# Dealing out the output projection between scores in a two-layer attention and gated-unit kernel

## The chip, the core and the metric

The kernel runs on one core of one Trainium2 chip. Its time is the device time in microseconds of one execution. Below, TensorE (PE) multiplies matrices, VectorE (DVE) and ScalarE (ACT) work on elements and may read PSUM, GpSimd (POOL) works on elements in SBUF and issues some DMAs, SyncE (SP) issues most DMAs. Each engine takes its own instructions in order. PSUM is where matmuls leave their sums; here it is used as eight banks of 128 x 512 float32.

## The reference

Two attention layers and two gated-unit layers alternate on x of 2048 rows and 448 columns. The weights of the two attention layers are the same, and so are those of the two gated units. There are 16 heads of 28 columns, which share one key and one value (multi-query attention).

```python
q = (x @ wq).reshape(B, S, H, Dh).transpose(0, 2, 1, 3)
k = x @ wk
v = x @ wv
p = _softmax(jnp.einsum("bhqd,bkd->bhqk", q, k) * (Dh ** -0.5))
attention = einsum("bhqk,bkd->bhqd", p, v) -> (B, S, H * Dh), then @ wo
unit = (_sigmoid(x @ w_gate) * (x @ w_up)) @ w_down

x = x + attention(_layernorm(x))
x = x + unit(_layernorm(x))
x = x + attention(_layernorm(x))
x = x + unit(_layernorm(x))
```

## The kernel before

**Precision.** Operands are split into a high and a low float16 part; a product is the sum of three of the four part products (high by high, high by low, low by high). Hence the output projection of one tile is 4 x 3 = 12 matmuls of 448 columns (line 625), and similar triples stand elsewhere.

**Tiles and steps.** The rows are 16 tiles of 128 (index `u`). The keys are 16 tiles of 128 (`kt`). A layer's attention is a loop of 16 x 16 steps. In a step, the order of the instructions is the string `ORDER = "FSFSFSFSPXM"`:

- `S`, four times: one score matmul of 128 keys by 4 heads x 128 rows into a PSUM bank (line 523), then the exponential on ScalarE into SBUF (line 526).
- `P`: the product with the values of the step before, eight TensorE records into one PSUM bank of its own (line 534).
- `X`: `tick()`, which counts down the stages of tiles whose attention is done, and issues those that are due; and the new rate of the filling work.
- `M`: one group of the row maxima of a later tile: four matmuls (line 493, `mx`), each into its bank, and four reductions on VectorE (line 497, `mp`).
- `F`, four times: `fill.slice`, which advances the count `now`, issues the work that was deferred (`defer`, `flush`), and then takes matmuls from the filling generators until a debt in ns is paid. The costs are constants (190 for 448 columns, 110 for 256, 216 for 512). The filling work is the gated unit of earlier rows (gate and up products `gp`, `up` at line 353, down products `dn` at line 716) and, in places, the query projection (`qp`).

**PSUM.** One bank holds the values' sums. The other seven have one tag, and all of `s`, `mx`, `gp`, `up`, `dn`, `qp`, `wo`, `mt` take theirs from it.

**Maxima.** The exponential needs each row's maximum ahead of the scores. It goes into the scores as row 28 of the query tile `QS`. When the 16 groups of a tile are done (24 for the first tile of the second layer), the generator `mx_gen` goes on at its next call: it reduces over the groups and scales (lines 506 and 507, `m32`, `m16`), puts a function `fin` into the list `late`, and begins the next tile's first group, ahead of which `fin` is called. `fin` transposes on TensorE (line 512, `mt`), copies on VectorE (line 514) and writes the row into `QS` by a DMA of GpSimd. `mx_gen` also issues the loads of `QH` (line 460) and the twelve loads of `QS` (line 449) on SyncE.

**After a tile's attention.** `Block.tile` (line 570) lists the stages of a tile with the number of steps to wait ahead of each: `f0` and `fx` store the row sums and load them in another shape; `fy` takes the reciprocal on VectorE (line 591); `fz` and `fw` store it and load it across the partitions; `fa` multiplies on GpSimd (line 608); `fb` splits into float16 parts on ScalarE and VectorE (lines 614, 615); `fc` is the output projection, twelve matmuls in one go, and defers the addition of the residual and the statistics (lines 630, 301, 302; then six operations on GpSimd); `fd` norms (lines 330, 322 to 324) and, for a block's second tile, loads the first two weight tiles; `fe` transposes by DMA (line 341); `ff` counts the tile as fed. Two tiles make a block; when both are fed, the block's gated unit becomes filling work. `FIRST` tells the planner at which step the first block is fed, and so how fast the filling has to go. What `tick()` issues directly (`fill.run`) is charged to the debt, which later slices pay by taking less.

In the first layer the weights are prepared beside all this (`paced`), and the stages `fa` and `fb` of its first four tiles wait two steps each. At a layer's end a loop of rounds (one `tick` and four slices) runs what is left; `KEEP` keeps filling work back for it.

Of the kernel before, what the change touches and what calls it, by code (L numbers as in the profile page):

```python
# [19 lines left out]
def interleaved_layers_kernel(ctx: ExitStack, tc: tile.TileContext, x, wq, wk, wv, wo, wg, wu, wd, out, layers=2):  # L20
# [45 lines left out]
    def defer(fn, lag=0):  # L66

        pend.append((now[0] + lag, fn))
# [11 lines left out]
    def fps(shape, dt, name):  # L80
        flush()
        return psf.tile(shape, dt, tag="f", name=name, bufs=NBK["f"])
# [92 lines left out]
    def need(n):  # L175

        if ready[0] < n:
            flush(True)
            while ready[0] < n:
                next(prep[0])  # L180
                prepd[0] += 1
                flush(True)
# [259 lines left out]
    def load_qs(l, u):  # L442
        b, t = divmod(u, 4)
        assert QDONE[l, b] == G
        q = wk1.tile([96, G, 4, 128], F16, name="QS", bufs=2)
        QS[l, u] = q
        for i, part in ((0, 0), (1, 0), (2, 1)):
            for g in range(G):
                nc.sync.dma_start(q[32 * i:32 * i + 32, g],
                                  qd[l % 2][b, g, part, :, t * 128:(t + 1) * 128].rearrange("(h d) n -> d h n", d=32))  # L450
# [25 lines left out]
    def mx_gen(l):  # L476

        load_qh(l, 0)
        for u in range(U):
            qh = QH[l, u]  # L480
            mp = wk1.tile([128, 4, 4, NB + 2], F32, name="mp", bufs=2)
            keys = ranges(l, u)
            for kb, (ka, kz) in enumerate(keys):
                for g in range(G):
                    for i in range(len(late) - 1, -1, -1):
                        late[i][0] -= 1
                        if late[i][0] <= 0:
                            late.pop(i)[1]()
                    assert KVD[l] * 128 >= kz
                    ps = [psf.tile([128, 512], F32, tag=BANKS["m"], name="mx", bufs=NBK[BANKS["m"]])  # L490
                          for _ in range(4)]
                    for h in range(4):
                        nc.tensor.matmul(ps[h][:, :kz - ka], qh[32 * h:32 * h + 32, g],  # L493
                                         KK[l][32 * h:32 * h + 32, 1, ka:kz], start=True,
                                         stop=True, tile_position=(32 * h, 0))
                    for h in range(4):
                        nc.vector.tensor_reduce(mp[:, g, h, kb:kb + 1], ps[h][:, :kz - ka], axis=AX.X, op=OP.max)  # L497
                    ps = None
                    if kz == S and g == 2 and u + 1 < U:
                        load_qh(l, u + 1)  # L500
                    if kb * 4 + g == 7:
                        load_qs(l, u)
                    yield
            m32 = wk1.tile([128, 16], F32, name="m32")
            m16 = wk1.tile([128, 16], F16, name="m16")
            nc.vector.tensor_reduce(m32, mp.rearrange("p g h k -> p (g h) k")[:, :, :len(keys)], axis=AX.X, op=OP.max)
            nc.vector.tensor_scalar(m16, m32, -(2.0 ** -15), None, op0=OP.mult)

            def fin(u=u, m16=m16):
                stored.add(("m", l, u))  # L510
                p = fps([16, 128], F16, "mt")
                nc.tensor.transpose(p, m16, id16)
                r = wk1.tile([16, 128], F16, name="mr")
                nc.vector.tensor_copy(r, p)
                nc.gpsimd.dma_start(QS[l, u][28:29].rearrange("o g h n -> o (g h) n"), r)
            late.append([LT, fin])
        while late:
            late.pop(0)[1]()

    def scores(l, u, kt, g, P):  # L520
        assert ("m", l, u) in stored, (l, u, kt)
# [39 lines left out]
    class Block:  # L561
# [8 lines left out]
        def tile(self, u):  # L570

            l, b = self.l, self.b
            t = u % TB
            v = {}

            def f0():
                v["o"] = PVS.pop((l, u))
                nc.sync.dma_start(sums[u % 2], v["o"][28:128:32])
                v["xr"] = wk1.tile([128, D], F32, tag="xr", name="xr", bufs=4)
                nc.sync.dma_start(v["xr"], x[0, u * 128:(u + 1) * 128] if l == 0 else x2d[u])  # L580
                return
                yield

            def fx():
                v["rc"] = wk1.tile([128, 16], F32, name="rc")
                nc.sync.dma_start(v["rc"], sums[u % 2].rearrange("g (a b) -> (g a) b", b=16))
                return
                yield

            def fy():  # L590
                nc.vector.reciprocal(v["rc"], v["rc"])
                return
                yield

            def fz():
                nc.sync.dma_start(sums[u % 2].rearrange("g (a b) -> (g a) b", b=16), v["rc"])
                return
                yield

            def fw():  # L600
                lb = v["lb"] = wk1.tile([128, 512], F32, name="lb", bufs=1)
                for g in range(G):
                    nc.sync.dma_start(lb[32 * g:32 * g + 32], sums[u % 2][g:g + 1].to_broadcast([32, 512]))
                return
                yield

            def fa():
                nc.gpsimd.tensor_tensor(v["lb"], v["o"], v["lb"], op=OP.mult)  # L608
                return
                yield  # L610

            def fb():
                oT = v["oT"] = wk1.tile([128, 2, 512], F16, name="oT")
                nc.scalar.copy(oT[:, 0], v["lb"])  # L614
                defer(lambda: nc.vector.tensor_tensor(oT[:, 1], v["lb"], oT[:, 0], op=OP.subtract))
                return
                yield

            def fc():
                need(1)  # L620
                p = fps([128, D], F32, "wo")
                n = 0
                for h in range(4):
                    for a, c in ((0, 0), (0, 1), (1, 0)):
                        nc.tensor.matmul(p, v["oT"][:, a, h * 128:(h + 1) * 128], WO[:, c, h], start=n == 0, stop=n == 11)  # L625
                        n += 1
                        yield C448

                def f():
                    nc.vector.scalar_tensor_tensor(self.x1[:, t], p, osc, v["xr"], op0=OP.mult, op1=OP.add)  # L630
                    v["ls"] = ln_stats(self.x1[:, t])[0]
                defer(f)

            def fd():
                if t == TB - 1:
                    self.load_w(0)
                    self.load_w(1)
                v["hl"] = ln_split(self.x1[:, t], *v["ls"], eng=nc.gpsimd)
                return
                yield  # L640

            def fe():
                if t == 0:
                    self.XT2 = wk1.tile([128, 7, TB * 128], F16, name="XT2")
                t7_dma(v["hl"], self.XT2, t)
                return
                yield

            def ff():
                self.fed += 1  # L650
                if self.fed == TB:
                    fill.add(self.bulk(), BULK)
                    if b == NBL - 1 and not self.last:
                        fill.add(qgen(l + 1, 1), G * QCH)
                return
                yield
            slow = 2 if l == 0 and u < 4 else 1
            return (1, f0), (1, fx), (1, fy), (1, fz), (1, fw), (slow, fa), (slow, fb), (2, fc), (2, fd), (3, fe), (2, ff)

        def load_w(self, f):  # L660
            need(2 + f)
# [111 lines left out]

    class Filler:
        def __init__(self):
            self.gens, self.debt = [], 0.0

        @property
        def left(self):
# [10 lines left out]
        def slice(self, ns):  # L790
            now[0] += 1
            flush()
            self.debt += ns
            while self.gens and self.debt > 0:
                g = self.gens[0]
                c = next(g[0], None)
                if c is None:
                    self.gens.remove(g)
                    continue
                self.debt -= c  # L800
                g[1] -= c
            if not self.gens:
                self.debt = min(self.debt, 0.0)
# [124 lines left out]
    early[0] = False  # L928
    ORDER = "FSFSFSFSPXM"
    MORE = (5, 10)  # L930
    FIRST = KT * TB + 16
    KEEP = 28000
    VS = 1800
    for l in range(layers):
        mx = mxs[l]
        final = l + 1 == layers
        next(mx, None)
        while late:
            late.pop(0)[1]()
        if not final:  # L940
            layer_tiles(l + 1)
        if l:
# [6 lines left out]
        for step in range(U * KT):  # L949
            u, kt = divmod(step, KT)  # L950
            P = []
            for o in ORDER:
                if o == "S":
                    scores(l, u, kt, len(P), P)
                elif o == "M":
                    for _ in range(1 + (u == 0 and kt in MORE)):
                        next(mx, None)
                elif o == "P":
                    if prevP is not None:
                        pv(*prevP)  # L960
# [55 lines left out]
```

## Time and profile before

| | |
|---|---|
| three runs | 2352.67, 2353.94, 2359.79 us; median 2353.94 |
| the profiled execution | 2352.99 us; from its first to its last instruction 2351.2 us |
| busy | TensorE 2241.4 us (95%), VectorE 1637.1 (70%), ScalarE 1568.9 (67%), GpSimd 335.0 (14%) |
| mean granted TensorE clock | 0.987 |
| exponentials (line 526) | 2048, 690 ns each |
| maxima reductions (line 497) | 2080, 674 ns each |
| score matmuls (line 523) | 2048, 382 ns each |
| output projection matmuls (line 625) | 384, 353 ns each |

The profile has one execution. A matmul's duration runs from its start to its modelled end, and successive matmuls overlap, so the distance from start to start is shorter than the duration. A row of the timeline is the start and duration in us, the engine (PEld is TensorE's weight load), the line, the operation, what it writes and reads with shapes, and how many such instructions it merges; behind it in brackets stands the time for which the engine had been idle, and what ended that. A row of the waits names who waited for whom, the total in us, how often, and the longest.

### The profile page before, as it was taken

Reading aid. Unit: us, or ns where it says so; the run is one execution under the profiler, and the core shown is the slowest. Engines: PE = TensorE matmul, PEld = TensorE weight load, DVE = VectorE, ACT = ScalarE, POOL = GpSimd, SP = SyncE. Lnnn points to the kernel's source line nnn. Section 1 sums busy time; section 2 is a strip of 40 time slices with the busy share of each in tenths; the row PEclk is TensorE's granted clock in tenths of the full one; section 3 lists DMA queues with packets and bytes.
Section 4 is the critical chain, followed back from the end, with each engine's and each line's share of the span. In section 5 each row is a group of like instructions: output and inputs, shape, how many; then the busy total and the mean of one; then the engine's idle time right before and its main releaser. Section 6 shows DMA issues by size and latency. Waiting matters only on the chain.

```text
span 2351.2 us, 41358 instructions
## 1 busy us (share of the span) xinstructions
PE 2241.4 (95%) x15786; PEld 1004.3 (43%) x15786; DVE 1637.1 (70%) x2941; ACT 1568.9 (67%) x2610; POOL 335.0 (14%) x606
## 2 busy tenths in 40 slices
PE   5898899999999999999999999999999999999999
PEld 3222243444444444444563224444344444444456
DVE  6887887777777777773467887777676777777321
ACT  6697776766667676777415777767676776777741
POOL 5203663100110110001101010000000000000010
PEclk9798999999999999999999999999999999999999
DMA  4243562323313132323341113223131323223133
GB/s 118 68 133 107 186 212 61 108 73 99 106 50 108 58 99 64 94 92 80 97 133 47 28 49 92 88 82 96 54 94 58 98 61 96 76 84 92 59 111 118
DMA packets 205639, 213.28 MB, mean 91 GB/s; under 512 B 137520, under 2 KB 165872, under 8 KB 205440
## 3 DMA queue, kind: packets, MB, share of 16 engines
q1 hardware_dynamic: 200064, 195.77, 28.7%
q0 software_dynamic: 5376, 14.87, 1.8%
q8 instruction: 123, 2.02, 0.4%
q14 instruction: 76, 0.62, 0.1%
HBM read 175.37 MB, written 23.59 MB: 85 GB/s over the span
## 4 chain that ended last, share of the span: by engine, by line
PE 52%; DVE 5%; DMA 1%; ACT 1%; issue 0%; SPq 0%; POOL 0%; ACTq 0%; DVEq 0%; POOLq 0%
PE pv L534 12%; PE s L523 10%; PE up L353 8%; PE gp L353 8%; PE dn L716 7%; PE mx L493 4%; DVE mp L497 4%; PE wo L625 2%; PE qp L353 1%; ACT P L526 1%; DMA wgu<-wgu_d 0%; DMA QH<-qd 0%; DMA sums<-rc 0%; DMA lb<-sums 0%; PE kv L353 0%
## 5 line engine op out<-in xcount | busy, mean ns | idle before, releaser
L526 ACT ACTIVATE P<-s,esc 128x512 f32<-128x512 f32 x2048 | 1310.0, 690 | 515.3 <-PE s L523 493.6
L497 DVE TENSOR_REDUCE mp<-mx 128x1 f32<-128x512 f32 (+1 forms) x2080 | 1270.8, 674 | 411.4 <-PE mx L493 407.8
L523 PE MATMUL s<-QS,KK 96*128 96x512 f16 x2048 | 762.8, 382 | 47.5 <-DVE mp L497 34.1
L353 PEld LDWEIGHTS <-wgu 128*128 128x128 f16 x4928 | 458.4, 98 | 241.7 <-issue 91.1
L534 PE MATMUL pv<-P,VV 128*32 128x512 f32 x4096 | 548.3, 608 | 0.0
L353 PE MATMUL gp<-XT,wgu 128*128 128x256 f16 x2464 | 374.9, 273 | 2.3 <-DMA wgu<-wgu_d 2.3
L353 PE MATMUL up<-XT,wgu 128*128 128x256 f16 x2464 | 376.2, 273 | 0.7 <-DVE mp L497 0.6
L716 PE MATMUL dn<-WD,h 128*128 128x448 f16 x1344 | 321.7, 353 | 0.0
L523 PEld LDWEIGHTS <-KK 96*128 96x128 f16 x2048 | 194.6, 97 | 170.4 <-issue 91.0
L493 PE MATMUL mx<-KK,QH 32*128 32x512 f16 (+1 forms) x2080 | 223.4, 388 | 11.2 <-DVE mp L497 3.7
L493 PEld LDWEIGHTS <-QH 32*128 32x128 f16 x2080 | 55.3, 91 | 384.6 <-issue 375.7
L716 PEld LDWEIGHTS <-h 128*128 128x128 f16 x1344 | 123.8, 98 | 136.7 <-issue 23.4
L534 PEld LDWEIGHTS pv<-P,VV 128*32 128x32 f32 x4096 | 81.1, 108 | 203.2 <-issue 191.1
L608 POOL TENSOR_TENSOR lb<-pvs,lb 128x512 f32<-128x512 f32 x32 | 40.5, 1266 | 761.9 <-DMA lb<-sums 666.8
L690 ACT ACTIVATE h<-th 128x512 f16<-128x512 f32 x112 | 70.2, 627 | 80.9 <-DVE th L687 80.9
L353 PE MATMUL qp<-XT,WQ 128*128 128x512 f16 x352 | 116.0, 401 | 1.3 <-DVE mp L497 0.8
L687 DVE SCALAR_TENSOR_TENSOR th<-th,up 128x512 f32<-128x512 f32 x112 | 76.0, 678 | 57.5 <-PE up L353 45.0
L679 ACT ACTIVATE th<-gp,gsc 128x512 f32<-128x512 f32 x112 | 76.8, 686 | 57.1 <-PE gp L353 57.1
L307 POOL TENSOR_SCALAR rs<-mv 128x1 f32<-128x1 f32 (+2 forms) x53 | 14.1, 265 | 702.2 <-DVE mv L302 698.1
L691 DVE SCALAR_TENSOR_TENSOR h<-th,h 128x512 f16<-128x512 f32 x112 | 77.2, 689 | 44.6 <-ACT h L690 44.6
L625 PE MATMUL wo<-WO,oT 128*128 128x448 f16 x384 | 78.4, 353 | 0.9 <-ACT oT L614 0.7
L353 PEld LDWEIGHTS <-WQ 128*128 128x128 f16 x352 | 34.2, 101 | 62.9 <-issue 40.6
(129 smaller groups left out, 841.9 us busy)
## 6 DMA issues: line engine op xcount, KB each, us to landing
wgu<-wgu_d SPq DMA_DIRECT2D x224, 512.0 KB
QS<-qd SPq DMA_DIRECT2D x384, 32.0 KB
lb<-sums SPq DMA_DIRECT2D x128, 64.0 KB
xr<-in_A_x_dram SPq DMA_DIRECT2D x32, 224.0 KB
qd<-qst POOLq DMA_DIRECT2D x28, 256.0 KB, 2.6
wgu_d<-sgu POOLq DMA_DIRECT2D x14, 512.0 KB, 3.9
QH<-qd SPq DMA_DIRECT2D x28, 128.0 KB
x2d<-x SPq DMA_DIRECT2D x16, 224.0 KB
```

Source lines behind the costliest of these rows:

```text
L353: nc.tensor.matmul(ps, a, b, start=n == 0, stop=n == 10)
L493: nc.tensor.matmul(ps[h][:, :kz - ka], qh[32 * h:32 * h + 32, g], KK[l][32 * h:32 * h + 32, 1, ka:kz], start=True, stop=True, tile_positio ...
L497: nc.vector.tensor_reduce(mp[:, g, h, kb:kb + 1], ps[h][:, :kz - ka], axis=AX.X, op=OP.max)
L523: nc.tensor.matmul(s, KK[l][0:96, 0, kt * 128:(kt + 1) * 128], QS[l, u][:, g].rearrange("p h n -> p (h n)"), start=True, stop=True)
L526: nc.scalar.activation(p, s, AF.Exp, scale=esc)
L534: nc.tensor.matmul(v[32 * g:32 * g + 32], VV[l][:, kt], P[g], start=kt == 0, stop=kt == KT - 1, tile_position=(0, 32 * g))
L625: nc.tensor.matmul(p, v["oT"][:, a, h * 128:(h + 1) * 128], WO[:, c, h], start=n == 0, stop=n == 11)
L679: defer(lambda: nc.scalar.activation(th, gp.rearrange("p j n -> p (j n)"), AF.Tanh, scale=gsc))
L687: nc.vector.scalar_tensor_tensor(t, th, 1.0, up.rearrange("p j n -> p (j n)"), op0=OP.add, op1=OP.mult)
L690: nc.scalar.activation(h[:, 0], t, AF.Copy, scale=2.0 ** -17)
L691: defer(lambda: nc.vector.scalar_tensor_tensor(h[:, 1], t, 2.0 ** -17, h[:, 0], op0=OP.mult, op1=OP.subtract), 1)
L716: nc.tensor.matmul(p, hs[f // 2][:, a, o:o + 128], WD[:, f, c], start=n == 0, stop=n == 3 * FC - 1)
```

## The change

Four edits. The stage `fc` no longer issues the twelve products; it hands a generator to the filler, which takes up to three of its products in each slice, ahead of other filling work and charged to the debt. The addition that reads their sum is deferred with the last product. `fd` waits three steps in place of two, and `FIRST` is one larger. The last reduction and scaling of the maxima are issued right behind a tile's last group, by a function `row_max`; `fin` keeps its place ahead of the next group, for which the calls at a layer's start and at the end of the generator are put in order. The reciprocal `fy` of the first layer's first four tiles waits two steps in place of one.

```diff
                     if kb * 4 + g == 7:
                         load_qs(l, u)
+                    if kz == S and g == G - 1:
+                        row_max(l, u, mp, len(keys))
                     yield
-            m32 = wk1.tile([128, 16], F32, name="m32")
-            m16 = wk1.tile([128, 16], F16, name="m16")
-            nc.vector.tensor_reduce(m32, mp.rearrange("p g h k -> p (g h) k")[:, :, :len(keys)], axis=AX.X, op=OP.max)
-            nc.vector.tensor_scalar(m16, m32, -(2.0 ** -15), None, op0=OP.mult)
-
-            def fin(u=u, m16=m16):
...
-            late.append([LT, fin])
-        while late:
-            late.pop(0)[1]()
+
+    def row_max(l, u, mp, n):
+
+        m32 = wk1.tile([128, 16], F32, name="m32")
+        m16 = wk1.tile([128, 16], F16, name="m16")
+        nc.vector.tensor_reduce(m32, mp.rearrange("p g h k -> p (g h) k")[:, :, :n], axis=AX.X, op=OP.max)
+        nc.vector.tensor_scalar(m16, m32, -(2.0 ** -15), None, op0=OP.mult)
+
+        def fin():
+            stored.add(("m", l, u))
+            p = fps([16, 128], F16, "mt")
+            nc.tensor.transpose(p, m16, id16)
+            r = wk1.tile([16, 128], F16, name="mr")
+            nc.vector.tensor_copy(r, p)
+            nc.gpsimd.dma_start(QS[l, u][28:29].rearrange("o g h n -> o (g h) n"), r)
+        late.append([LT, fin])
...
             def fc():
+                fill.first.append(wo_products())
+                return
+                yield
+
+            def wo_products():
                 need(1)
                 p = fps([128, D], F32, "wo")
                 n = 0
+
+                def f():
+                    nc.vector.scalar_tensor_tensor(self.x1[:, t], p, osc, v["xr"], op0=OP.mult, op1=OP.add)
+                    v["ls"] = ln_stats(self.x1[:, t])[0]
                 for h in range(4):
                     for a, c in ((0, 0), (0, 1), (1, 0)):
                         nc.tensor.matmul(p, v["oT"][:, a, h * 128:(h + 1) * 128], WO[:, c, h], start=n == 0, stop=n == 11)
                         n += 1
+                        if n == 12:
+                            defer(f)
                         yield C448
-
-                def f():
-                    nc.vector.scalar_tensor_tensor(self.x1[:, t], p, osc, v["xr"], op0=OP.mult, op1=OP.add)
-                    v["ls"] = ln_stats(self.x1[:, t])[0]
-                defer(f)
...
-            return (1, f0), (1, fx), (1, fy), (1, fz), (1, fw), (slow, fa), (slow, fb), (2, fc), (2, fd), (3, fe), (2, ff)
+            return (1, f0), (1, fx), (slow, fy), (1, fz), (1, fw), (slow, fa), (slow, fb), (2, fc), (3, fd), (3, fe), (2, ff)
...
-            self.gens, self.debt = [], 0.0
+            self.gens, self.debt, self.first = [], 0.0, []
...
             self.debt += ns
+            for _ in range(3):
+                c = next(self.first[0], None) if self.first else None
+                if c is None:
+                    self.first[:1] = []
+                    break
+                self.debt -= c
             while self.gens and self.debt > 0:
...
-    FIRST = KT * TB + 16
+    FIRST = KT * TB + 17
...
-        next(mx, None)
         while late:
             late.pop(0)[1]()
+        next(mx, None)
...
-                        next(mx, None)
+                        if next(mx, "end") == "end" and late:
+                            late.pop(0)[1]()
```

More of the change, by code (lines that the diff above doesn't have):

```diff
@@ L502, in mx_gen @@
                         load_qs(l, u)
+                    if kz == S and g == G - 1:
+                        row_max(l, u, mp, len(keys))
                     yield
-            m32 = wk1.tile([128, 16], F32, name="m32")
-            m16 = wk1.tile([128, 16], F16, name="m16")
-            nc.vector.tensor_reduce(m32, mp.rearrange("p g h k -> p (g h) k")[:, :, :len(keys)], axis=AX.X, op=OP.max)
-            nc.vector.tensor_scalar(m16, m32, -(2.0 ** -15), None, op0=OP.mult)
-            def fin(u=u, m16=m16):
[L510 to L515, printed above, removed]
-            late.append([LT, fin])
-        while late:
-            late.pop(0)[1]()
+    def row_max(l, u, mp, n):
[11 more added lines that the diff above has]
+        late.append([LT, fin])
     def scores(l, u, kt, g, P):
```

## The prediction

> **What bounds the kernel now.** I read the head of the page first, then TensorE's waits, then the timeline around one output projection, because the changed products run there.
>
> ```profile
> span 2351.2 us, 41358 instructions
> ...
> PE 2241.4 (95%) x15786; PEld 1004.3 (43%) x15786; DVE 1637.1 (70%) x2941; ACT 1568.9 (67%) x2610; POOL 335.0 (14%) x606
> ```
>
> TensorE is busy 95% of the span and idle for 110 us. Whatever shortens the kernel must take something out of those 110 us, since no product is removed. The waits say who ends them:
>
> ```profile
> PE s L523 <- DVE mp L497: 34.1, 108, 0.9
> PE mt L512 <- DVE m L507: 17.0, 13, 3.7
> ...
> DVE rc L591 <- DMA rc<-sums: 12.1, 4, 4.9
> ```
>
> The reader is to see two waits that this change touches: scores (s) that wait for a maxima reduction (mp) to give a PSUM bank back, 34.1 us, and the transposed row of maxima (mt) that waits for its own input (m), 17.0 us. Here is one output projection on TensorE (start, duration, what, idle before):
>
> ```profile
> 1526.94 2.44 PE L625 MATMUL wo<-WO,oT 128*128 128x448 f16 x12
> 1529.31 0.39 PE L493 MATMUL mx<-KK,QH 32*128 32x512 f16 x4
> 1529.64 0.39 PE L523 MATMUL s<-QS,KK 96*128 96x512 f16 x1
> 1530.48 0.38 PE L523 MATMUL s<-QS,KK 96*128 96x512 f16 x1 [0.45 <-DVE mp L497]
> 1531.08 0.59 PE L523 MATMUL s<-QS,KK 96*128 96x512 f16 x2 [0.22 <-DVE mp L497]
> 1531.60 1.06 PE L534 MATMUL pv<-P,VV 128*32 128x512 f32 x8
> 1532.60 0.40 PE L493 MATMUL mx<-KK,QH 32*128 32x512 f16 x4
> 1532.93 0.39 PE L523 MATMUL s<-QS,KK 96*128 96x512 f16 x1
> 1533.15 0.54 PE L716 MATMUL dn<-WD,h 128*128 128x448 f16 x2
> ...
> 1535.23 1.06 PE L534 MATMUL pv<-P,VV 128*32 128x512 f32 x8
> ```
>
> The twelve products run in one burst of 2.4 us, and the planner then owes that time: the next step, 1529.31 to 1532.60, has no filling work at all. Its pieces, by starts: mx to s 0.33, three spacings of s at 0.21 (the last row of two, 0.59 less 0.38), s to pv 0.31, pv to mx 1.00; 2.28 us in all. It took 3.29. So 1.0 us is lost there, of which the idle figures show 0.67 because a matmul's own 0.38 covers the rest. The burst has another 0.09: wo to mx is 2.37 for twelve products at 0.19 (two dn plus one s take 0.60 in the step after). **The price of one burst is 1.09 us.** The loss comes from banks: four mx, the output sum, the open filling sum and the first s make seven, so the second s waits for the first maxima reduction.
>
> **The change part by part.**
>
> *Products dealt out.* The same 12 loads and 12 matmuls go three at a time ahead of the four scores of the next step. Three products (0.57) ahead of each score are what ordinary filling puts there, so that step costs its work, and the second score comes at 0.33+0.57+0.21+0.57 = 1.68 after the mx; the bank is given back 1.17 after it (1529.31 to 1530.48). No wait. The debt after four slices is the same as before, so the step after it has the pattern of the 1532.60 step: nothing ahead of the first score, two dn ahead of the second. But the bank of the output sum is now still held there, because the addition that reads it is deferred past the next maxima:
>
> ```profile
> 1529.74 2.48 DVE L497 TENSOR_REDUCE mp<-mx 128x1 f32<-128x512 f32 x4 [3.90 <-PE mx L493]
> 1532.14 0.68 DVE L630 SCALAR_TENSOR_TENSOR x<-wo,osc,xr 128x448 f32<-128x448 f32 x1
> ```
>
> It ends 3.5 us after the mx, as it did, but a step later. The second score could start at 0.33+0.21+0.38 = 0.92 and gets its bank at 1.17: 0.25 lost. With one gate or up product (0.11) in place of two dn it would be 0.65, so 0.52 lost; where the planned rate is higher (the first layer's middle) nothing. I take 0.35, between 0 and 1.09 (the whole wait moves there). 28 of the 32 projections are followed by a step with maxima (the last two of each layer are not): 28 x (1.09 - 0.35) = **20.7 us**, bounds 0 and 30.5.
>
> [...]
>
> *Maxima's last steps.* The final reduction and scaling (m) are issued a step earlier, behind their last group; the transpose, its copy and the row's DMA stay where they were. Before, everything queued on VectorE stood ahead of m while TensorE waited:
>
> ```profile
> 258.83 0.74 DVE L131 SCALAR_TENSOR_TENSOR sgu<-rgu,swb,sgu 128x512 f16<-128x512 f32 x1
> ...
> 260.34 0.21 DVE L506 TENSOR_REDUCE m<-mp 128x16 f32<-128x64 f32 x1
> 260.59 0.74 DVE L507 TENSOR_SCALAR m<-m 128x16 f16<-128x16 f32 x1
> ```
>
> ```profile
> 261.38 0.22 PE L512 MATMUL mt<-id,m 128*16 128x128 f16 x1 [2.83 <-DVE m L507]
> ```
>
> The same waits by stretches, 80 to 96 us, 190 to 410 us and 1250 to 1265 us:
>
> ```profile
> PE mt L512 <- DVE m L507: 3.7, 1, 3.7
> ```
>
> ```profile
> PE mt L512 <- DVE m L507: 9.2, 4, 2.8
> ```
>
> ```profile
> PE mt L512 <- DVE m L507: 1.7, 1, 1.7
> ```
>
> The first and the last are at a layer's start, where nothing stands between group and transpose: they stay. The four of the first layer's first tiles are 9.2 us; the remaining seven are 17.0-3.7-1.7-9.2 = 2.4. In the changed order m is done about 0.43+2.48+0.4 = 3.3 us after its mx, and TensorE needs more than 4 us with the products in that step, so the transpose does not wait. What is late next: VectorE's queue itself (the same sgu, and the norm's work), so mx and s may wait for banks. I take half of the 9.2, **4.6**, and all of the 2.4; bounds 2.4 and 11.6.
>
> After two of these four the clock was halved:
>
> ```profile
> 197.80:208.10 10.30, 9.69 (x39) 2.04 (x39) 6.42 (x16) 4.97 (x8) 1.79 (x3) 0.50 0.12 23
> 262.70:266.10 3.40, 3.39 (x14) 0.42 (x13) 1.75 (x3) 2.07 (x4) 3.32 (x4) 0.50 0.36 142
> ```
>
> ```profile
> 200.87 1.94 PE L534 MATMUL pv<-P,VV 128*32 128x512 f32 x8
> ...
> 206.19 1.93 PE L534 MATMUL pv<-P,VV 128*32 128x512 f32 x8
> ...
> 275.34 1.07 PE L534 MATMUL pv<-P,VV 128*32 128x512 f32 x8
> ...
> 278.35 1.07 PE L534 MATMUL pv<-P,VV 128*32 128x512 f32 x8
> ```
>
> The column before the last two is the granted clock, 0.50. A step without filling took 5.32 there and 3.01 at full clock (275.34 to 278.35): 2.3 us. At most half of 10.3+3.4 is lost, 6.9; I take **3.0** as saved, bounds 0 and 6.9.
>
> [...]
>
> *Reciprocals.* A step later for the first layer's first four tiles only. The waits have 12.1 us for VectorE, but three of the four lie in a layer's last steps or its tail, where VectorE has no maxima to reduce; one counts:
>
> ```profile
> 155.44 1.06 PE L534 MATMUL pv<-P,VV 128*32 128x512 f32 x8
> ...
> 158.51 1.07 PE L534 MATMUL pv<-P,VV 128*32 128x512 f32 x8
> ...
> 161.66 0.25 DVE L591 RECIPROCAL rc<-rc 128x16 f32<-128x16 f32 x1 [2.32 <-DMA rc<-sums]
> ...
> 162.87 0.64 PE L534 MATMUL pv<-P,VV 128*32 128x512 f32 x4
> ```
>
> That step took 4.36 us (158.51 to 162.87), the one before it 3.07: **1.3** saved. The store of the reciprocals stood ahead of the twelve QS loads on SP's queue and now stands behind them, 6.5 us:
>
> ```profile
> 161.94 0.33 SPq L596 DMA_DIRECT2D sums<-rc  x1
> 162.37 6.47 SPq L449 DMA_DIRECT2D QS<-qd  x12
> ```
>
> The row sums then come 6.5 us less one step later; the product with the row sums on POOL has two steps of room and ScalarE's copy two more, so nothing waits. If that cover were gone, ScalarE would stand still for the difference, some 2 us four times.
>
> *Later norm.* Addition, statistics (VectorE), six POOL operations, xn and hl, the two weight loads and the transposing DMA on SP all come a step later, with the same distances between them. The weight loads of odd tiles fall behind the QH load on SP in place of ahead of it. From the fifth tile on, the planner's constant moves with it, 16 to 17. For the first two blocks the delay grows by two and the constant by one, so each has one more step without filling: 3.01 - 2.28 = 0.7 each, **1.4 lost**. In a layer's tail one more round is run; TensorE is covered there:
>
> ```profile
> 2282.18 15.49 PE L716 MATMUL dn<-WD,h 128*128 128x448 f16 x81
> 2297.50 2.57 PE L353 MATMUL gp<-XT,wgu 128*128 128x256 f16 x22
> ```
>
> 81 products, 15.5 us, stand between the last projection and the first product that needs the normed row. I cost it at nothing; without that cover it is a round, which the planner sets at 1.8 us, in each layer.
>
> **Sum:** 20.7 + 4.6 + 2.4 + 3.0 + 1.3 - 1.4 = 30.6. The profiled execution took 2352.99 (span 2351.2), so 2322.4; it lies 0.95 under the median of the three runs, 2353.94, so **2323.3**.
>
> **The rivals.**
> 1. *Everything is saved*: no residue in the following step and all maxima waits and 4.5 of the clock gone: 30.5+11.6+4.5+1.3-1.4 = 46.5, 2307.4. For it: steps with enough filling show no idle time between 1532.93 and 1535.23. Against: the late addition.
> 2. *VectorE is the bound in the first layer's start*: the early maxima waits return as bank waits, and the clock still drops: 20.7+2.4+1.3-1.4 = 23.0, 2330.9. For it: sgu and the reductions stand in one queue at 258 to 261. Against: VectorE is busy 70%.
> 3. *The bank wait moves on*: the step after the products loses 0.9 in place of 0.35: 28 x 0.19 = 5.3, in all 15.2, 2338.7. For it: four mx, output sum, open sum and one s again make seven.
> 4. *Slower*: with the output sum held over two steps, both starve; each loses the 1.09 that one lost. 28 x (1.09 - 2.18) = -30.5, with the other 9.9 of the sum 20.6 slower, 2374.5. It decides from 1.09+9.9/28 = 1.44 lost per projection. Against: three products cover the first of the two steps.
> 5. *It doesn't reach the end*: the lost time is only VectorE's and ScalarE's pace in other dress, and each wait comes back elsewhere: about 2353.
>
> **Chances.** Forecast 0.55 (its own range 2314 to 2331), rival 1 0.10, 2 0.12, 3 0.12, 4 0.05, 5 0.06. The range 2308 to 2342 takes in rivals 1 to 3 nearly whole and leaves out 4 and 5. About 0.3% (7 us) is what a measurement can tell from no change: the forecast and rivals 1 to 3 are faster by more, 0.89; rival 5 is no change, 0.06; rival 4 slower, 0.05.
>
> **What would show it.** Right: wo in groups of three between scores; the waits of s for mp fall from 34.1 to 20 or less; mt for m falls to about 5.4 (the two layer starts); clock 1.00 from 198 to 208; the reciprocal at tile 1 without 2.3 us of idle time. The residue is one wait of about 0.25 (dn) or 0.5 (gate, up) in the second step behind each projection. Wrong: waits of s or mx for mp as long as before but a step later (rivals 2, 3), in both steps (4), or new waits of gp for XT or wgu in the tails.

## The result and the profile after

| | before | changed |
|---|---|---|
| median of 6 runs each | 2355.3 us (2352.67 to 2359.79) | 2334.88 us (2331.55 to 2343.67) |
| profiled execution, its span | 2352.99, 2351.2 | 2331.55, 2329.8 |
| mean granted clock | 0.987 | 0.988 |

The ratio is 0.9917, with a 95% interval from 0.9897 to 0.9937. The change gains 20.4 us of the 30.6 that were forecast; 2334.88 lies within the range (2308 to 2342) and above the forecast's own (2314 to 2331).

The head of the changed kernel's page and its waits (who waited for whom, total us, times, longest):

```profile
span 2329.8 us, 41404 instructions
...
PE 2229.5 (96%) x15786; PEld 1007.1 (43%) x15786; DVE 1643.0 (71%) x2941; ACT 1584.2 (68%) x2610; POOL 335.6 (14%) x606
```

```profile
PE s L526 <- DVE mp L497: 22.8, 78, 1.0
...
DVE rc L594 <- DMA rc<-sums: 18.7, 9, 5.3
...
PE s L526 <- ACT P L529: 17.9, 34, 3.2
...
PE mt L517 <- DVE m L512: 7.7, 6, 3.7
```

Scores wait 11.3 us less for maxima reductions (34.1 before) and the transpose 9.3 us less (17.0). The third row is new in weight: scores that wait for an exponential to give its bank back, 17.9 us where the page before had 9.5 (24 times, none over 0.8). ScalarE has begun to hold TensorE up. The second row concerns VectorE: its waits for the row sums, which the fourth edit was to shorten, grew from 12.1 us (4 times) to 18.7 (9 times). The longest new one, 5.32 us, ends at 1079.98 us, near the end of the first layer, where no wait of TensorE stands (1068 to 1092 us).

One output projection among down products, on TensorE:

```profile
2027.70 1.06 PE L537 MATMUL pv<-P,VV 128*32 128x512 f32 x8
2028.69 0.40 PE L493 MATMUL mx<-KK,QH 32*128 32x512 f16 x4
2029.02 0.74 PE L637 MATMUL wo<-WO,oT 128*128 128x448 f16 x3
2029.60 0.38 PE L526 MATMUL s<-QS,KK 96*128 96x512 f16 x1
2029.82 0.73 PE L637 MATMUL wo<-WO,oT 128*128 128x448 f16 x3
...
2032.27 1.07 PE L537 MATMUL pv<-P,VV 128*32 128x512 f32 x8
...
2033.60 0.39 PE L526 MATMUL s<-QS,KK 96*128 96x512 f16 x1
2033.83 0.54 PE L725 MATMUL dn<-WD,h 128*128 128x448 f16 x2
2034.44 0.38 PE L526 MATMUL s<-QS,KK 96*128 96x512 f16 x1
...
2036.13 0.64 PE L537 MATMUL pv<-P,VV 128*32 128x512 f32 x4
```

From here on a step's **loss** is its length, from one pv to the next, less its work: 2.28 for what is in every step, 0.19 for each wo or dn, 0.11 for each gate or up product (four in a row take 0.60 and three 0.49, at 1438.39 and 1437.84), 0.22 for each query product (two in a row take 0.60 and one 0.38, at 257.41 and 258.62); a step without maxima has 0.33 less, and the few transposes and the key and value products are taken off too. The step with the twelve products takes 4.57 (2027.70 to 2032.27) for 2.28 + 12 x 0.19 = 4.56: no loss, where one burst lost 1.09. The step behind it takes 3.86 for 2.28 + 7 x 0.19 = 3.61 and loses 0.25; its second score comes 0.84 after the first (2033.60 to 2034.44) in place of 0.59.

The losses of all steps, added by stretch (steps counted through both layers, 16 to a tile; the last two columns are kernels of the experiments below):

| steps | before | changed | split a slice later | both corrections, reciprocal back |
|---|---|---|---|---|
| 1 to 26 | 17.5 | 16.6 | 16.6 | 19.6 |
| 27 to 46 (first projection, first filling) | 23.5 | 11.8 | 11.9 | 13.4 |
| 47 to 80 | 14.1 | 10.6 | 8.9 | 10.5 |
| 81 to 96 (the first layer's tile 5) | 2.5 | 8.0 | 8.8 | 3.1 |
| 97 to 128 | 6.0 | 3.0 | 2.8 | 2.5 |
| 129 to 255 | 17.1 | 12.5 | 7.1 | 6.2 |
| between the layers, to 304 | 46.8 | 48.6 | 48.2 | 47.1 |
| 305 to 512 | 19.7 | 13.6 | 7.2 | 2.5 |
| sum | 147.2 | 124.7 | 111.4 | 104.9 |

The sum falls by 22.5, the span by 21.4. Most comes where the first maxima waits were (27 to 46: 11.7) and evenly over the rest of both layers; 5.5 us is given back in one place, steps 81 to 96, and the second layer gains 6.1 where the prediction's 0.74 for each of its 12 projections in that stretch makes 8.9.

In the second layer the tiles with down products gain what was forecast and the others hardly anything. Mean losses over ten of its tiles, five of each kind (the step in the tile in brackets):

| | before | changed |
|---|---|---|
| down: ahead of the products, with them, behind | 0 (8), 1.10 (9), 0 (10) | 0.10 (8), 0.01 (9), 0.24 (10) |
| gate, up: the same, and one earlier step | 0.33 (4), 0.21 (7), 1.10 (9), 0.30 (10) | 0.33 (5), 0.79 (8), 0.01 (9), 0.56 (10) |

Here is such a loss of 0.79, in the timeline of TensorE, VectorE and ScalarE around a gate tile's step ahead of the products:

```profile
1438.04 1.29 ACT L529 ACTIVATE P<-s,esc 128x512 f32<-128x512 f32 x2 [0.80 <-PE s L526]
...
1439.67 0.68 DVE L618 TENSOR_TENSOR oT<-lb,oT 128x512 f16<-128x512 f32 x1
...
1440.27 0.68 DVE L696 SCALAR_TENSOR_TENSOR th<-th,up 128x512 f32<-128x512 f32 x1
...
1440.80 0.58 PE L493 MATMUL mx<-KK,QH 32*128 32x512 f16 x4
1440.99 0.63 ACT L699 ACTIVATE h<-th 128x512 f16<-128x512 f32 x1 [1.65 <-DVE th L696]
...
1441.52 2.48 ACT L529 ACTIVATE P<-s,esc 128x512 f32<-128x512 f32 x4
...
1442.25 0.38 PE L526 MATMUL s<-QS,KK 96*128 96x512 f16 x1 [0.44 <-ACT P L529]
```

VectorE subtracts the projection's low part (oT, line 618) and only then makes th. ScalarE's next instruction is h, the high part of th; it stands still 1.65 us for it, with the exponentials of two finished scores queued behind. Their banks are not given back, and the score at 1442.25 comes 1.45 after the mx at 1440.80, where 0.33 + 3 x 0.11 = 0.66 is its work: 0.79 lost. Before the change th did not stand behind oT, because the gated unit then began one step earlier against the projection. In the kernel before, in a tile of this kind:

```profile
1453.35 0.68 DVE L687 SCALAR_TENSOR_TENSOR th<-th,up 128x512 f32<-128x512 f32 x1
...
1457.73 0.68 DVE L615 TENSOR_TENSOR oT<-lb,oT 128x512 f16<-128x512 f32 x1
```

There th comes a step ahead of oT, and that step loses the 0.21 of the table.

### The profile page after: what moved, and what is told of

It reads as the page before. It is cut to its first block, busy times and chain, and to the rows that moved or that the text cites. A ratio compares the mean times of both kernels' runs of the same rounds, so it can differ in the third digit from the quotient of the medians.

```text
span 2329.8 us, 41404 instructions
## 1 busy us (share of the span) xinstructions
PE 2229.5 (96%) x15786; PEld 1007.1 (43%) x15786; DVE 1643.0 (71%) x2941; ACT 1584.2 (68%) x2610; POOL 335.6 (14%) x606
## 4 chain that ended last, share of the span: by engine, by line
PE 82%; DVE 8%; ACT 3%; issue 2%; DMA 1%; SPq 1%; POOL 0%; DVEq 0%; ACTq 0%; POOLq 0%
PE pv L537 19%; PE s L526 17%; PE up L353 11%; PE dn L725 11%; PE gp L353 11%; PE mx L493 7%; DVE mp L497 6%; PE wo L637 3%; PE qp L353 2%; ACT P L529 2%; DVE th L696 0%; DVE oT L618 0%; PE kv L353 0%; DMA rc<-sums 0%; DMA wgu_d<-sgu 0%
## 5 line engine op out<-in xcount | busy, mean ns | idle before, releaser
L526 PE MATMUL s<-QS,KK 96*128 96x512 f16 x2048 | 767.0, 381 | 43.8 <-DVE mp L497 22.8
L537 PEld LDWEIGHTS pv<-P,VV 128*32 128x32 f32 x4096 | 80.9, 108 | 204.4 <-issue 199.3
L637 PE MATMUL wo<-WO,oT 128*128 128x448 f16 x384 | 93.1, 352 | 1.1 <-ACT oT L617 0.9
```

The lines of the kernel that those rows point to most:

```text
L526: nc.tensor.matmul(s, KK[l][0:96, 0, kt * 128:(kt + 1) * 128], QS[l, u][:, g].rearrange("p h n -> p (h n)"), start=True, stop=True)
L537: nc.tensor.matmul(v[32 * g:32 * g + 32], VV[l][:, kt], P[g], start=kt == 0, stop=kt == KT - 1, tile_position=(0, 32 * g))
```

## The experiments

Each kernel is timed against the kernel before, run beside it. Numbers with "under" or "over" are differences of medians.

**The dealing alone.** The kernel before with the twelve products dealt out, the norm a step later and the larger constant; maxima and reciprocals as before.

```diff
-            return (1, f0), (1, fx), (1, fy), ... (2, fc), (2, fd), (3, fe), (2, ff)
+            return (1, f0), (1, fx), (1, fy), ... (2, fc), (3, fd), (3, fe), (2, ff)
```

> The kernel before with the products dealt out and the norm a step later alone; the maxima's last steps and the reciprocals as before. My theory: this part carries most of the change. The step with the products loses no more than 0.1 us (1.09 before), the step after it 0.24 in tiles whose filling is down products and about 0.5 in tiles whose filling is gate and up products. The maxima's transposed row waits less too, since the norm's work no longer stands ahead of it on VectorE: its waits fall from 17.0 to about 11 us. In all 12 to 18 us faster than before. Rival (the maxima's early issue does the work, the dealing only moves the waits): at most 8 us faster.

2341.67 us, ratio 0.9947 (0.993 to 0.9965): 13.1 under the kernel before. TensorE's waits in it:

```profile
PE s L523 <- DVE mp L497: 27.3, 81, 1.9
PE mt L512 <- DVE m L507: 17.3, 13, 3.6
```

The waits for the maxima's last steps stay whole (17.3 against 17.0); that part of the expectation was wrong. The table of second-layer losses above comes out the same in this kernel, 0.79, 0.56 and 0.24 included, so they belong to this part.

**The maxima alone.** The kernel before with the last reduction and scaling behind their group.

```diff
+                    if kz == S and g == G - 1:
+                        row_max(l, u, mp, len(keys))
                     yield
```

> The kernel before with the maxima's last reduction and scaling issued right behind their last group, and nothing else. My theory: the four long waits of the transposed row in the first layer's first tiles (9.2 us) go, the two at the layers' starts (5.4 us) stay, the half clock behind 198 us goes: 6 to 10 us faster. Rival (VectorE's queue is what is late, the wait comes back as waits of scores and maxima for banks): 0 to 3 us faster, with those waits up by some 6 us.

2344.06 us, ratio 0.9955 (0.994 to 0.997): 10.8 under, a little more than expected.

```profile
PE s L526 <- DVE mp L497: 34.6, 108, 1.0
PE s L526 <- ACT P L529: 9.5, 24, 0.8
PE mt L517 <- DVE m L512: 9.1, 8, 3.7
```

The transpose's waits fall by 7.9 and do not come back as bank waits: 34.6 for maxima against 34.1, 9.5 for exponentials as before. No half clock stands near 198 us in it; the mean granted clock of that execution is 0.988.

**The reciprocals alone.**

```diff
-            return (1, f0), (1, fx), (1, fy), ...
+            return (1, f0), (1, fx), (slow, fy), ...
```

> The kernel before with the reciprocals of the first layer's first four tiles a step later, and nothing else. My theory: VectorE's 2.3 us wait for the row sums near 161 us goes, worth 1.3 us; each of the first two blocks is fed one step later, which costs 0.7 each: no difference in time (within 3 us). Rival (the later feeding makes stages of two tiles meet on one queue, as near 411 us in the changed kernel): 3 to 6 us slower, with a wait of over 2 us of scores for ScalarE between 400 and 430 us.

2357.3 us over ten runs, ratio 1.0012 (1.0002 to 1.0021): 2.5 us *slower*, within the 3 us expected. The rival's sign is not there: no wait of a score for ScalarE is longer than 1.2 us. In its trace steps 47 to 80 lose 6.4 more than before, but that execution took 2361.19, 8.2 more than the profiled one before, so not all of it can be the edit's. One transposing step there, with a norm ahead of it on VectorE (a row of the clock, below, has the stretch, its length, the busy time of the engines from TensorE on, then the granted clock, DMA share and GB/s):

```profile
398.75 0.48 DVE L330 TENSOR_SCALAR xn<-x,mv,rs 128x448 f32<-128x448 f32 x1
...
400.72 0.18 DVE L507 TENSOR_SCALAR m<-m 128x16 f16<-128x16 f32 x1
...
400.96 0.27 PE L512 MATMUL mt<-id,m 128*16 128x128 f16 x1 [3.15 <-DVE m L507]
```

The same transpose in the kernel before:

```profile
400.14 0.22 PE L512 MATMUL mt<-id,m 128*16 128x128 f16 x1 [1.88 <-DVE m L507]
```

And the half clock behind it with the later reciprocals:

```profile
400.00:406.80 6.80, 5.84 (x19) 2.24 (x20) 4.37 (x11) 1.92 (x3) 2.94 (x7) 0.50 0.19 37
```

A norm stood ahead of the maxima's last steps at this place before as well, that of tile 3 (its xn at 398.84), and TensorE waited 1.88 us. With the later reciprocals tile 3's norm has moved on by a step, but its addition and statistics (397.28 to 398.83) and the norm of the first block's finished output, which the second layer reads, are there in its place: TensorE waits 3.15 us and runs 6.8 us at half clock. How much of the 2.5 us comes from this step, one trace does not tell.

The three parts alone give 13.1 + 10.8 - 2.5 = 21.4; together they gave 20.4. They add.

**The burst kept, behind the maxima.** The changed kernel, but all twelve products in one slice, ahead of the step's first score; before the change they stood ahead of the maxima.

```diff
-            for _ in range(3):
+            for _ in range(12):
```

> The changed kernel, with up to twelve products in a slice in place of three: the burst is whole again, but it stands behind the maxima's matmuls and ahead of the first score, where the kernel before had it ahead of the maxima. My theory (the price of the burst is the wait for banks that VectorE has not yet given back): the burst gives VectorE 2.3 us for its reductions, so no score waits in that step; its loss is at most 0.2 us and the time is that of the changed kernel within 4 us. Rival (a burst of any place starves ScalarE and VectorE, and the dealing out is what cures it): the loss of 1 us for each of 28 projections is back, some 20 us slower than the changed kernel, that is about the time of before.

2334.23 us, ratio 0.9912 (0.9895 to 0.9928): the same as the changed kernel. Dealing out is not what gains. What gains is that the products stand between a step's maxima matmuls and its scores, so that the reductions run under them; how many stand ahead of each score makes no difference to the time. The step behind loses less here (0 and 0.28 in place of 0.24 and 0.56), since the last product, and with it the addition, comes earlier. Steps 305 to 512 lose 3.1 less for it than in the changed kernel's trace; steps 47 to 80 lose 5.8 more, a stretch that varies between traces (see the next run), and whether the 3.1 are worth anything is not shown by the times.

**The changed kernel again**, beside the next three.

> The changed kernel once more, beside the next three: 0.988 to 0.995 of the time before, by any theory.

2334.35 us, ratio 0.9913 (0.9897 to 0.9929). The losses of its trace differ from those of the first in steps 27 to 46 (13.2 and 11.8), 47 to 62 (10.0 and 6.8) and between the layers (51.8 and 48.6); in all other stretches they agree to 0.1. Steps 1 to 26 vary as well: the kernel with the fifth reciprocal, below, loses 1.4 more there, ahead of its edit. Differences of that size in those four stretches are therefore not read as an edit's doing.

**The addition ahead of the maxima.** The changed kernel with the addition that reads the output sum issued right behind the step's value products, ahead of the next four maxima reductions.

```diff
                         if n == 12:
-                            defer(f)
+                            soon.append(f)
...
                         pv(*prevP)
+                    add_now()
```

> The changed kernel, with the addition that reads the products' sum (and the statistics behind it) issued behind the values' product, ahead of the next maxima on VectorE, in place of behind them. My theory: the residue in the step behind the products (0.24 us in down tiles, 0.45 to 0.6 in gate tiles, 28 tiles) is the sum's bank, held until the addition; given back before the maxima take theirs, the residue falls below 0.1 and the kernel is 5 to 9 us faster than the changed one. Rival (1.5 us of addition and statistics ahead of the maxima make these late in turn): the loss stays at 0.2 to 0.6, within 3 us of the changed kernel or slower.

2329.74 us, ratio 0.989 (0.9875 to 0.9905): 4.6 under the changed kernel (2334.35), a little less than expected. The step behind the products loses 0 in both kinds of tile, 0.79 and 0.33 stay. So the 0.24 and 0.56 were the output sum's bank, held behind four reductions.

**The split a slice later.** The changed kernel with ScalarE's h issued three slices after th in place of two.

```diff
-                    defer(parts, 2)
+                    defer(parts, 3)
```

> The changed kernel, with the gated unit's split on ScalarE (h) issued a slice later behind its product on VectorE (th). My theory: the losses that the changed kernel has new, 0.8 to 0.95 us at step 8 of gate tiles and 1.1 to 1.3 at step 13 of three first-layer tiles, are ScalarE standing in h for th, which VectorE reaches late because the output's split (oT) or the early maxima (m) now stand ahead of it in that step; the exponentials behind h are late and keep their banks. A slice later, h finds th done: these losses fall to 0.3 or less and the kernel is 6 to 11 us faster than the changed one. Rival (VectorE itself is the bound there): within 2 us of the changed kernel.

2321.0 us, ratio 0.9857 (0.984 to 0.9873): 13.3 under the changed kernel, more than expected. ScalarE's idle time ahead of h (busy us and mean ns, then idle us and what ended it), in the kernel before, the changed one and this one:

```profile
L690 ACT ACTIVATE h<-th 128x512 f16<-128x512 f32 x112 | 70.2, 627 | 80.9 <-DVE th L687 80.9
```

```profile
L699 ACT ACTIVATE h<-th 128x512 f16<-128x512 f32 x112 | 70.3, 627 | 93.7 <-DVE th L696 93.6
```

```profile
L699 ACT ACTIVATE h<-th 128x512 f16<-128x512 f32 x112 | 70.0, 625 | 63.5 <-DVE th L696 63.4
```

The 0.79 falls to 0.13, the 0.33 and the 0.10 to 0. The rows show that ScalarE stood 80.9 us ahead of h before the change already; the change added 12.8. One slice of room takes away 30.2, more than the change had cost, in both layers (5.4 in steps 129 to 255, 6.4 in the second layer).

**The reciprocal of the fifth tile too.** The changed kernel with the later reciprocal for the first five tiles, to mend steps 81 to 96. What happens there in the changed kernel, at tile 5:

```profile
405.49 2.63 SPq L341 DMA_TRANSPOSE XT<-hl  x2
408.22 0.53 SPq L589 DMA_DIRECT2D rc<-sums  x1
...
410.08 0.25 DVE L594 RECIPROCAL rc<-rc 128x16 f32<-128x16 f32 x1 [1.79 <-DMA rc<-sums]
410.25 0.43 DVE L330 TENSOR_SCALAR xn<-x,mv,rs 128x448 f32<-128x448 f32 x1
...
410.71 0.56 ACT L322 CAST hl<-xn 128x448 f16<-128x448 f32 x1 [2.85 <-DVE xn L330]
...
411.18 2.42 ACT L529 ACTIVATE P<-s,esc 128x512 f32<-128x512 f32 x4
...
411.91 0.38 PE L526 MATMUL s<-QS,KK 96*128 96x512 f16 x1 [3.19 <-ACT P L529]
```

Tile 3's transposing DMA, two steps later than before (one by the reciprocal, one by the norm), now falls into the step of tile 4's load of the row sums. It stands on SP's queue ahead of that load, together with one for the first block's finished output. Tile 4's reciprocal is not one of the four that wait longer; it comes while its load is under way, VectorE waits 1.79 for it with the next norm of that output (xn) behind, ScalarE waits 2.85 for xn with four exponentials behind, and TensorE 3.19 for the first of these.

> The changed kernel, with the reciprocals of the first layer's fifth tile a step later too. My theory: the 3.2 us wait of a score near 411 us and the half clock behind it come from that reciprocal, which stands on VectorE for its row sums, whose load stands behind two transposing DMAs on SyncE's queue since the fourth tile's stages moved by two steps; a step later it finds them: 4 to 5 us faster than the changed kernel. Rival (the wait goes on to the next instruction in the queue): within 1.5 us of the changed kernel, with a wait of 2 us or more still there.

2334.42 us, ratio 0.9911 (0.9897 to 0.9926): no gain; a miss. The step that lost 3.5 loses 1.5 and the half clock behind it is gone, but two steps behind it lose 1.9 and 0.8, so the stretch of steps 81 to 96 falls by 2.0 only (8.0 to 6.0), which the spread of the times (2333.39 to 2337.43) does not show.

**The reciprocal back.** The changed kernel without its fourth edit.

```diff
-            return (1, f0), (1, fx), (slow, fy), ...
+            return (1, f0), (1, fx), (1, fy), ...
```

> The changed kernel with the reciprocal back at one step behind its load; the rest of the change stays. If the later reciprocal costs here what it cost alone (2.5 us): 2 to 3 us faster than the changed kernel, near 2332, and the 3.19 us wait of a score for an exponential near 412 us is gone, because tile 4's transposing loads are not behind tile 3's any more. Rival: its price depends on what happens to meet it, and with the other edits in place it makes no difference, 2334 to 2335; the 3.19 us wait then stays, since what put tile 3's transposing DMAs ahead of tile 4's loads is a delay of two steps and one of them is the norm's.

2336.15 us, ratio 0.9911 (0.9897 to 0.9924): no difference, though the 3.19 us wait is gone, as the first theory has it (scores wait 1.2 us in all for exponentials between 400 and 425 us, 3.6 in the changed kernel). Tile 1 loses again what the edit had saved there (its step takes 4.40 in place of 3.15). The price of this edit was not resolved in this kernel.

**Both corrections**: the addition ahead and the split later.

> The changed kernel with both corrections: the addition issued ahead of the next maxima's reductions, and the low parts of the gated unit's h split one slice later. If the bank held by the late addition and ScalarE's wait for VectorE's th are separate losses, the gains add: 4.6 and 13.3 make 17.9, some 2316 to 2318. Rival: they are one loss in two places (VectorE's queue), then little is gained over the later split alone, 2320 to 2322.

2314.48 us, ratio 0.9825 (0.9811 to 0.9838): 20.4 under the changed kernel's 2334.88, against 17.9 for the sum of the two. They are separate losses. The second layer's steps 305 to 512 lose 2.5 in all.

**Both corrections and the reciprocal back.**

> Both corrections, and the reciprocal back at one step. If the reciprocal's later step costs 2.5 us whatever stands around it: 2 to 3 us under the kernel with both corrections and the later reciprocal. Rival: no difference between the two within 1.5 us.

2309.15 us, ratio 0.9801 (0.9787 to 0.9814): 5.3 under the kernel with both corrections, about twice what was expected; their ranges do not meet (2305.06 to 2311.07, 2312.38 to 2315.71). It is the fastest kernel of this study, 46.9 us under the kernel before. TensorE's waits for exponentials with the later reciprocal, and the half clock behind them, and then the same without it:

```profile
PE s L531 <- ACT P L534: 9.4, 17, 3.4
```

```profile
413.60:417.00 3.40, 3.39 (x25) 0.88 (x24) 2.63 (x7) 1.97 (x5) 0.00 (x0) 0.53 0.27 59
```

```profile
PE s L531 <- ACT P L534: 7.1, 14, 1.3
```

```profile
411.00:418.00 7.00, 6.22 (x60) 3.06 (x53) 5.71 (x14) 4.42 (x10) 0.77 (x4) 1.00 0.70 208
```

**Both corrections and five later reciprocals.**

> Both corrections, and the reciprocal a step later for the first five tiles in place of four. The later fifth reciprocal gained nothing with the changed kernel (the half clock at 414 us went, losses of the same size came in the steps behind). The same is expected here: within 1.5 us of the kernel with both corrections. If the half clock at 414 us were worth its length, 3 to 5 us less.

2311.49 us, ratio 0.9813 (0.9799 to 0.9826): 3.0 under the kernel with both corrections and four, ranges apart (2310.62 to 2312.22). Within 1.5 was expected: a miss. Of the kernels with both corrections, the two that clear the stall at 412 us are faster than the one that has it.

## Why the prediction was right, and where it was wrong

By its own terms, against what each part gave alone:

| | forecast | measured alone |
|---|---|---|
| products dealt out and later norm (20.7 - 1.4) | 19.3 | 13.1 |
| maxima and clock (4.6 + 2.4 + 3.0) | 10.0 | 10.8 |
| reciprocals | 1.3 | -2.5 |
| sum | 30.6 | 21.4 |

**Products: price and residue right, mechanism half right.** The 1.09 of a burst is gone from its step (4.57 for 4.56), and the residues that were read off the bank's times, 0.25 and 0.52, measured 0.24 and 0.56. That they are the output sum's bank is shown by the kernel with the addition ahead, where both are 0; giving it back ahead of the maxima was worth 4.6 us there (2334.35 to 2329.74). The kernel that keeps the burst shows that the order was the cause and the dealing was not. Rival 4, in which holding the bank costs more than the burst, would have needed 1.44.

**Later norm: the step that failed.** It "come[s] a step later, with the same distances between them", and was costed at nothing but the 1.4 at the start. Among the moved instructions the distances held. The work that the norm feeds did not stay where it was: a block's gated unit begins a step later, and the split of the *next* projection's operand (lines 617 and 618), which did not move, now meets its th. That is the 0.79 of the gate tiles, where the kernel before lost 0.21, one step earlier. The kernel that keeps the burst loses the 0.79 too, so it does not come from the dealing; the norm's step alone, without the products moved, was not tried. The gate tiles gain 1.94 - 1.69 = 0.25 each, by the table above, where the down tiles gain 1.10 - 0.35 = 0.75 and the forecast took 0.74 for all. Rival 3 had the size for those tiles but another place: the wait moved to the step ahead of the products, and it is ScalarE that waits.

**Maxima: right.** The transposes' waits fell from 17.0 to 7.7 (5.4 was named, and the two layer starts have it, 3.7 and 1.7; the rest are four short waits, none over 0.9) and the bank waits that rival 2 put in their place did not come: alone, the part left them at 34.6. Half of the 9.2 had been kept back for that. The edit has VectorE do 0.4 us of its work a step earlier; alone, it gave TensorE one new kind of wait for VectorE, 1.5 us in all for the copy of the transposed row (mr).

**Clock: right at its place.** This is the changed kernel where the clock was halved for 10.3 us before, and two later stretches:

```profile
198.00:208.00 10.00, 8.10 (x55) 2.09 (x51) 9.18 (x23) 8.13 (x15) 4.95 (x6) 1.00 0.04 5
...
259.70:263.10 3.40, 3.40 (x12) 0.51 (x10) 1.88 (x4) 1.37 (x2) 1.87 (x4) 0.50 0.39 154
413.30:416.70 3.40, 3.40 (x25) 1.87 (x26) 3.40 (x8) 1.68 (x5) 0.00 (x0) 0.50 0.28 61
```

A drop near 260 us stayed, and one came at 413.30, behind the new wait of 3.19. In the kernel before there was a third stretch at 0.50, from 225.1 to 228.5 us, which the prediction does not name; it is gone too. What the clock gave by itself was not separated from the maxima's 10.8.

**Reciprocals: the sign was wrong.** At tile 1 the saving is there:

```profile
158.99 1.07 PE L537 MATMUL pv<-P,VV 128*32 128x512 f32 x8
...
162.06 1.06 PE L537 MATMUL pv<-P,VV 128*32 128x512 f32 x8
...
162.81 0.24 DVE L594 RECIPROCAL rc<-rc 128x16 f32<-128x16 f32 x1
...
165.21 1.06 PE L537 MATMUL pv<-P,VV 128*32 128x512 f32 x8
```

The reciprocal has no idle time ahead of it and its step takes 3.15 in place of 4.36. But "so nothing waits" looked only at the row sums of the same tile. Everything behind the reciprocal moves too, the norm and the transposing DMA, and the prediction did not follow them to tile 4, whose reciprocal is not delayed. Alone the edit costs 2.5 us, in the changed kernel nothing that can be measured, and 5.3 with both corrections. Why the changed kernel hides it is open. The one trace of the kernel with the reciprocal back loses 4.7 less in steps 81 to 96, but 3.1, 4.7 and 4.2 more in steps 1 to 26, 27 to 46 and between the layers, and its time, 2343.12, was the longest of its five; whether the edit causes those losses was not tried.

The forecast that the scores' waits for maxima "fall from 34.1 to 20 or less" was missed by 2.8 (22.8). No new waits for XT or weight tiles stand in the tails.

## What to carry to other kernels

When a step of a pipeline is moved, list not only what moves with it but what it feeds, and look for unmoved work that the fed work now meets on the same engine: here one subtraction of 0.68 us, ahead of th, held up ScalarE (1.65 us ahead of h at 1440.99), its queued exponentials and so PSUM banks (0.79 us lost in that step). A product that needs no fresh data was well placed here between the matmuls whose results are being reduced and the next that need their banks (13.1 us for the dealing alone); a burst there took the same time here as pieces (2334.23 and 2334.88 us). Where an engine is seen idle ahead of an instruction with ready work queued behind it (80.9 us ahead of h in the profile *before*), issuing that instruction one slot later is the cheapest thing to try: it gave 13.3 us here on the changed kernel, as much as the largest part of the change.

## What the runs showed of the hardware

The clock of the changed kernel fell once without a long wait ahead of it. These are the 3.4 us ahead of its drops at 259.70 and 413.30, and, second, 3.4 us that no drop follows (length, then TensorE's busy us first):

```profile
256.30:259.70 3.40, 1.94 (x11) 0.68 (x8) 2.68 (x5) 2.49 (x5) 1.02 (x2) 1.00 0.02 5
406.50:409.90 3.40, 2.22 (x16) 0.54 (x16) 1.79 (x3) 1.35 (x3) 1.16 (x5) 1.00 0.75 145
409.90:413.30 3.40, 1.39 (x12) 0.24 (x12) 2.59 (x7) 2.59 (x5) 0.00 (x0) 1.00 0.16 34
```

In the first, the longest single wait of TensorE is 0.56 us. The half clock behind each of the two drops lasted 3.4 us; it lasted 10.3 us from 197.8 in the kernel before and 6.8 us from 400.0 in the one with the later reciprocals. In these three rows the less busy stretches were followed by half clock (1.39 and 1.94 of 3.40) and the busier one was not (2.22). But busy time alone does not decide. In the kernel before, 1.87 busy (221.71 to 225.12) was followed by half clock and 1.85 (324.11 to 327.52) by full clock. This stretch of the dealing alone has a single wait of 1.94 us in it, and full clock behind it:

```profile
330.40:333.80 3.40, 1.54 (x11) 0.97 (x10) 3.40 (x5) 1.75 (x4) 2.66 (x4) 1.00 0.01 1
```

In the same trace a stretch with 2.85 busy (129.00 to 132.40) was followed by half clock, and in the changed kernel one with 2.77 (48.07 to 51.48). What decides was not shown.

Two traces of one kernel, the changed one, lose 13.63 and 13.66 us in the second layer's steps 305 to 512, and 7.99 and 8.03 in steps 81 to 96, but 6.8 and 10.0 in steps 47 to 62. Its times reach from 2331.55 to 2343.67. What varies sits at the first layer's start and between the layers; an edit there has to be worth several microseconds to be seen, one in the second layer can be read from a single trace.
